# A new order of instructions for a three-stage attention, gMLP and expert-attention kernel, with k's high part copied twice from PSUM and scaled weight words on either of two engines

## The chip, the cores and the metric

One core of one Trainium2 chip runs the program. The metric is the device time of one execution in microseconds (us). Engines are named as in the profile: PE is TensorE (matmuls and transposes), DVE is VectorE, ACT is ScalarE, POOL is GpSimd, SP is SyncE, which issues every load and store here.

## What is computed

Three stages run one after the other on a batch of 4 sequences of 576 positions with 512 features (8 heads of 64):

```python
# (a) attention in a window of 64 positions
scores = scale * np.matmul(q, k.transpose(0, 1, 3, 2))
mask = (rel >= 0) & (rel < window)          # rel = query position - key position
attn = softmax(np.where(mask, scores, -1e9)); x = attn @ v
# (b) gated MLP with a mix over positions
h = np.maximum(x @ w_in, 0.0); u, v = h[..., :512], h[..., 512:]
v_n = (v - mu) / np.sqrt(var + 1e-06)
v_s = np.einsum('ts,bsd->btd', w_spatial, v_n) + b_spatial[None, :, None]
x = (u * v_s) @ w_out
# (c) four experts, causal attention each (head 64); each position keeps its two best by logits
logits = x @ w_gate; w = normalised exp of the two best logits, 0 for the others
for e in range(4):
    a = softmax(causal(scale * (x @ wq[e]) @ (x @ wk[e]).T)); out += w[e] * (a @ (x @ wv[e]) @ wo[e])
```

Inputs and output are float32. The kernel splits many operands into a high and a low part (names ending in h and l: xh and xl, woh and wol, kd with kz for k) and adds two or three matmuls for one product.

## The kernel before

**The planner.** The code first describes the work as nodes: an engine (or several that could do it, with a cost on each), a function that emits the instructions, the nodes it depends on, and the tiles that it allocates and uses. A class `Planner` (`N = plan.node`) is a list scheduler: in `run` it goes forward in planned time, and whenever an engine is free it starts there the ready node of lowest priority number. Priorities are running sums of work, moved by the table `SHIFT`, one number for each unit of work and kind (PE, other engines, loads). `SWITCH` is a penalty for changing between full-array and tiled matmuls on PE; `DVE_BIAS`, `POOL_BIAS` and `EFT` decide which engine takes a node that several could do; `RATE` is the planned speed of loads; `CLASH` makes DVE and POOL wait for each other in the plan where both work in SBUF (`sbuf=True`). The costs are only for planning. The resulting order is written out as it stands: each engine executes its list in order and waits by semaphores. All loads and stores stand on SP's queue.

**Two plans.** Phase 1 holds (a), (b) and the folding of w_out into the weights of (c); phase 2 holds (c). Each ends in `plan.run()`. Phase 2 begins in PE's queue some 280 us after the start.

**The front.** Stage (a) goes by couples of score units. PE multiplies scores into a bank of PSUM (`s_mm`, matmuls of 64x128, first operands vt, ut or kt); DVE adds the mask and takes the extremum (`s_top`, L546, into pa, and mx for the row values); ACT exponentiates (`s_exp`, L552); DVE adds and inverts (L568, L570); DVE, POOL or ACT multiply by the inverse (`s_norm`, L558 on ACT, L560 otherwise); PE transposes (`p_t`, L564, "T" below); ACT or DVE copy the result to SBUF (pt); PE multiplies by v (`pv`, pt with woh and wol, or with vt, into a bank); ACT or DVE write xh, DVE subtracts for xl (L357). When all xh and xl of 128 positions are there, PE can do a b_v unit (12 matmuls of 128x512, `w,xh` and `w,xl`: v of the MLP). Four of these and a short one for the last 64 positions stand in the front, then the first b_u unit (`xh,w`, 128x288). From there PE has matmuls of stage (b) ready at all times.

**Weights.** The helper `prep64` takes weights as pairs of 32-bit words: `down` scales one word into a bank (L679, ACT), `sign` masks it (L674 and L676), and DVE shifts and joins (L688 to L696); then a copy makes the high part and a subtraction the low part.

**Dummies.** PE's first instructions are `WARM` dummy matmuls (`heat`, ident by ident, each leaves two records in the trace), and 60 single ones (`FILL`) have the worst priority, so that the planner puts one wherever it finds nothing else for PE. There are 68 with `WARM = 8`.

**Phase 2.** `c_qk` makes q and k of an expert: `hi` copies each half of k's high part from PSUM to kd, `lo` subtracts for the low part, and `twin` copies kd once more to the other half of the partitions (64x288 each). `c_v` makes v and, with it, the gate's logits (`w,xh` 128x260, "gate-and-v unit" below). `unit` is a block of causal softmax: scores (`kd,qs` and `kz,qs`), L1207 on DVE, exponent on ACT (L1218), L1220 to L1222 on DVE or POOL (p times the inverse and the gate), transposes on PE (L1238) and a copy to pg. `c_pv` multiplies by v, and `c_wo` by wo, copies the bank to a tile of ot, of which there are three, and stores it. For one block (`b == B - 1 and t == 1`) it does this in two halves of 256 columns. The layernorm of (b) has its small steps at L766 to L772.

## Time and profile before

| what | value |
|---|---|
| time, median of 3 runs | 447.91 us (447.51 to 448.07) |
| the profiled execution | 448.94 us, its span 447.1 us |
| PE busy | 438.9 us (98%), 3962 matmul records |
| DVE busy | 310.9 us (70%) |
| ACT busy | 293.1 us (66%) |
| POOL busy | 107.4 us (24%) |
| clock granted to PE | full (1.00) over the whole span |

The span runs from the first instruction to the last landing; the profiled execution's time has 1.84 us around it. An engine's busy share is a mean over stages that differ, so the rows below go by stretches. A timeline row begins with its start in us and its length; in brackets stands how long the engine idled before it and what ended the idling. Rows that follow each other on an engine can overlap, as instructions are pipelined.

### The profile page before, as it was taken

Reading aid. Unit: us, or ns where it says so; the run is one execution under the profiler, and the core shown is the slowest. Engines: PE = TensorE matmul, PEld = TensorE weight load, DVE = VectorE, ACT = ScalarE, POOL = GpSimd, SP = SyncE. Lnnn points to the kernel's source line nnn. Section 1 sums busy time; section 2 is a strip of 40 time slices with the busy share of each in tenths; the row PEclk is TensorE's granted clock in tenths of the full one; section 3 lists DMA queues with packets and bytes.
Section 4 is the critical chain, followed back from the end, with each engine's and each line's share of the span. In section 5 each row is a group of like instructions: output and inputs, shape, how many; then the busy total and the mean of one; then the engine's idle time right before and its main releaser. Section 6 shows DMA issues by size and latency. Waiting matters only on the chain.

```text
span 447.1 us, 10829 instructions
## 1 busy us (share of the span) xinstructions
PE 438.9 (98%) x3962; PEld 396.0 (89%) x3962; DVE 310.9 (70%) x1241; ACT 293.1 (66%) x926; POOL 107.4 (24%) x154
## 2 busy tenths in 40 slices
PE   8999999999999999999999999999999999999996
PEld 7977899989899879998899999789899978897875
DVE  4989989962875988024544556998697987787650
ACT  4989989662676969203322346987675978777863
POOL 4335782400310126000200251610031011011110
PEclk9999999999999999999999999999999999999999
DMA  7994837140242605003001000000010001000114
GB/s 280 281 330 122 251 101 221 45 140 0 64 138 64 179 7 144 0 1 95 1 1 48 0 1 1 1 2 1 1 48 25 1 2 48 0 2 25 71 53 160
DMA packets 31079, 33.10 MB, mean 74 GB/s; under 512 B 1905, under 2 KB 24689, under 8 KB 31026
## 3 DMA queue, kind: packets, MB, share of 16 engines
q1 hardware_dynamic: 31026, 32.41, 23.4%
q8 instruction: 31, 0.51, 0.5%
q14 instruction: 22, 0.18, 0.1%
HBM read 27.68 MB, written 4.72 MB: 72 GB/s over the span
## 4 chain that ended last, share of the span: by engine, by line
PE 87%; DVE 6%; ACT 4%; issue 2%; POOL 1%; POOLq 0%; ACTq 0%; DVEq 0%
PE bank L333 79%; PE bank L1238 5%; PE bank L564 3%; DVE p L1207 1%; ACT pa L552 1%; DVE qs L357 1%; POOL p L1222 1%; DVE p L1222 1%; ACT p L1218 1%; DVE pa L546 0%; ACT pa L558 0%; DVE pa L560 0%; DVE kz L357 0%; ACT pg L344 0%; ACT kd L344 0%
## 5 line engine op out<-in xcount | busy, mean ns | idle before, releaser
L333 PE MATMUL bank<-xh,w 128*128 128x288 f32 x512 | 109.6, 298 | 0.0
L333 PEld LDWEIGHTS bank<-xh,w 128*128 128x128 f32 x512 | 84.1, 188 | 0.9 <-DVE st L767 0.2
L333 PE MATMUL bank<-xl,w 128*128 128x288 f32 x256 | 75.3, 294 | 0.0
L333 PE MATMUL bank<-w,xh 128*128 128x512 f32 (+1 forms) x256 | 64.7, 342 | 0.2 <-ACT pt L344 0.2
L552 ACT ACTIVATE pa<-pa,mx 128x128 f32<-128x128 f32 x144 | 55.9, 400 | 5.4 <-DVE mx L546 5.4
L333 PEld LDWEIGHTS bank<-xl,w 128*128 128x128 f32 x256 | 48.2, 188 | 0.4
L333 PEld LDWEIGHTS bank<-w,xh 128*128 128x128 f32 x256 | 43.2, 188 | 5.7 <-ACT pt L344 0.5
L1218 ACT ACTIVATE p<-p,mc 128x128 f32<-128x128 f32 (+4 forms) x72 | 41.8, 582 | 8.4 <-DVE mc L1207 7.7
L1222 POOL TENSOR_SCALAR p<-p,mc,fx 128x256 f32<-128x256 f32 (+4 forms) x26 | 17.1, 658 | 111.3 <-DVE mc L1221 52.2
L333 PE MATMUL bank<-w,xl 128*128 128x512 f32 (+1 forms) x128 | 43.2, 338 | 0.0
L333 PE MATMUL bank<-wsp_h,vh 128*128 128x288 f32 x128 | 38.6, 302 | 0.0
L333 PE MATMUL bank<-wsp_h,vl 128*128 128x288 f32 x128 | 37.7, 295 | 0.0
L333 PE MATMUL bank<-wsp_l,vh 128*128 128x288 f32 x128 | 37.7, 294 | 0.0
L1207 DVE CUSTOM_DVE_ANT_0 p<-bank,cmask 128x128 f32<-128x128 f32 (+4 forms) x72 | 33.2, 482 | 5.2 <-PE bank L333 4.2
L770 POOL TENSOR_TENSOR st<-st,nhalf 128x1 f32<-128x1 f32 (+1 forms) x20 | 12.3, 615 | 98.7 <-DVE st L769 98.7
L344 ACT ACTIVATE pg<-bank 128x128 f32<-128x128 f32 (+4 forms) x71 | 29.1, 440 | 5.2 <-PE bank L1238 4.7
L546 DVE CUSTOM_DVE_ANT_0 pa<-bank,mask 128x128 f32<-128x128 f32 x120 | 28.4, 284 | 5.9 <-POOL mx L415 4.1
L1238 PE MATMUL bank<-ident,p 128*128 128x128 f32 x192 | 30.1, 278 | 1.5 <-POOL p L1222 0.7
L333 PE MATMUL bank<-kd,qs 128*128 128x128 f32 (+5 forms) x96 | 30.5, 335 | 0.0
L552 ACT ACTIVATION_READ_ACCUMULATOR pa<-pa,mx 128x1 f32 x144 | 28.6, 199 | 0.0
L333 PE MATMUL bank<-kz,qs 128*128 128x128 f32 (+5 forms) x96 | 28.4, 313 | 0.0
L835 DVE TENSOR_TENSOR y<-bank,ut 128x288 f32<-128x288 f32 x24 | 10.9, 454 | 24.9 <-PE bank L333 24.9
(209 smaller groups left out, 1083.4 us busy)
## 6 DMA issues: line engine op xcount, KB each, us to landing
vt<-in_v_dram SPq DMA_DIRECT2D x12, 512.0 KB, 4.9
qa<-in_qT_dram SPq DMA_DIRECT2D x44, 96.0 KB, 3.8
out_dram<-ot SPq DMA_DIRECT2D x15, 256.0 KB, 2.0
y<-in_w_in_dram SPq DMA_DIRECT2D x7, 512.0 KB, 7.3
kt<-in_kT_dram SPq DMA_DIRECT2D x12, 288.0 KB, 5.0
y<-in_w_outT_dram SPq DMA_DIRECT2D x4, 512.0 KB, 4.5
y<-in_wspT_dram SPq DMA_DIRECT2D x2, 576.0 KB, 4.2
vt<-in_kq_dram SPq DMA_DIRECT2D x2, 384.0 KB, 4.4
```

Of the source, the lines that this page charges most:

```text
L333: pe.matmul(o, lhsT, rhs, start=start, stop=stop)
L344: act.activation(o, i, AF.Copy)
L357: engs[e].tensor_tensor(out=o, in0=a, in1=hi.bitcast(F32), op=ALU.subtract)
L546: dve.tensor_tensor_reduce(out=pa[:, j, :], in0=ps[:, j * 128:(j + 1) * 128], in1=mask(j), scale=-0.125, scalar=3.0e38, op0=ALU.add, op1=A ...
L552: act.activation(pa[:, j, :], pa[:, j, :], AF.Exp, bias=mx[:, j, 0:1], scale=-1.0, accum_out=mx[:, j, 1:2])
L564: pe.transpose(ps2[:, j * 128:(j + 1) * 128], pa[:, j, :], ident)
L770: a = N((POOL, 464), lambda e: pool.tensor_tensor(out=st[:m, 9:10], in0=st[:m, 8:9], in1=nhalf[:m], op=ALU.pow), [n1], use=[st])
L835: dve.tensor_tensor(out=o, in0=ps[:, :HS], in1=u[:, d, tk], op=ALU.mult)
L1207: dve.tensor_tensor_reduce(out=P[:, a0:a1], in0=ps[:, :w], in1=msk, scale=-0.125, scalar=3.0e38, op0=ALU.add, op1=ALU.min, accum_out=mc[:, ...
L1218: a = N((ACT, 284 + 0.87 * L), lambda e: act.activation(P[:m, :L], P[:m, :L], AF.Exp, bias=mc[:m, 0:1], scale=-1.0, accum_out=mc[:m, 2:3]) ...
L1222: a = N({POOL: 328 + 0.832 * L, DVE: 90 + 0.52 * L}, lambda e: engs[e].tensor_scalar(P[:, :L], P[:, :L], mc[:, 3:4], fx[:, I, ev:ev + 1], ...
L1238: pe.transpose(ps[:, j * m:(j + 1) * m], P[:, j * 128:(j + 1) * 128], ident)
```

## The change

- Tables and constants: `SHIFT` (all numbers), `SWITCH`, `DVE_BIAS`, `POOL_BIAS`, `EFT`, `RATE` (360 to 328) are replaced, `WARM` goes from 8 to 4, and some planning costs (the first `s_mm`, `s_norm`, a `tensor_reduce`) and `sbuf` flags of the plan change. None of these alters an instruction; they alter the order, the engine that takes a node, and the number of dummies.
- `twin` reads k's high part from the PSUM bank (ps) where it read kd in SBUF.
- `down` may also run on DVE, as a `tensor_scalar` with two multiplications.
- In the layernorm the operation that negates the mean (L769 before) is gone; the last operation subtracts the mean where it added its negative.

```diff
-SWITCH = 107920.0
+SWITCH = 147606.0
...
-DVE_BIAS = (1136.0, 1147.0)
-POOL_BIAS = (1131.0, 1068.0)
-WARM = 8
+DVE_BIAS = (156.0, 2438.0)
+POOL_BIAS = (1196.0, -5786.0)
+WARM = 4
...
-EFT = (636.0, 778.0)
+EFT = (1480.0, 9505.0)
...
-    ISSUE, WAY, RATE, FLIGHT = 475.0, 650.0, 360.0, 8
+    ISSUE, WAY, RATE, FLIGHT = 475.0, 650.0, 328.0, 8
...
-        S_N[n0] = S_N[n0 + 1] = top = N((PE, 816), s_mm, kn + [Q_N[n0], Q_N[n0 + 1], S_N.get(n0 - 1)], alloc=bank, use=hk, prio=prio,
+        S_N[n0] = S_N[n0 + 1] = top = N((PE, 816 if n0 else 1500), s_mm, kn + [Q_N[n0], Q_N[n0 + 1], S_N.get(n0 - 1)], alloc=bank, use=hk, prio=prio,
...
-            a = N({POOL: 1053, DVE: 450, ACT: 880}, s_norm, [a], use=[pa, mx], prio=prio, sbuf=True)
+            a = N({POOL: 955, DVE: 468, ACT: 880}, s_norm, [a], use=[pa, mx], prio=prio, sbuf=True)
...
         def down(e):
-            act.activation(fb.t, word(1).bitcast(F32), AF.Copy, scale=2.0 ** -112)
+            if e == ACT:
+                act.activation(fb.t, word(1).bitcast(F32), AF.Copy, scale=2.0 ** -112)
+            else:
+                dve.tensor_scalar(fb.t, word(1).bitcast(F32), 2.0 ** -112, 1.0, op0=ALU.mult, op1=ALU.mult)
...
-        n1 = N((ACT, 550), down, [n0], alloc=[fb], use=[raw], prio=prio)
+        n1 = N({ACT: 550, DVE: 602}, down, [n0], alloc=[fb], use=[raw], prio=prio)
...
-        n2 = N((DVE, 70), lambda e: dve.tensor_scalar(st[:m, 10:11], st[:m, 6:7], -1.0, None, op0=ALU.mult), [a], use=[st])
...
         a = N({DVE: 460, POOL: 850}, lambda e: engs[e].tensor_scalar(
-            vr[:m], vr[:m], st[:m, 10:11], st[:m, 9:10], op0=ALU.add, op1=ALU.mult), [a, n2], use=[vr, st], sbuf=True)
+            vr[:m], vr[:m], st[:m, 6:7], st[:m, 9:10], op0=ALU.subtract, op1=ALU.mult), [a], use=[vr, st], sbuf=True)
...
             def twin(e):
                 for x in range(2):
-                    copy(e, kd[x][HALF[1 - x], tk], kd[x][HALF[x], tk])
+                    copy(e, kd[x][HALF[1 - x], tk], ps[HALF[x], :HS])
...
-            n3 = N(halves(HS, False), twin, [n1], use=kd, sbuf=True)
+            n3 = N(halves(HS), twin, [n1], use=[ps] + kl + kd)
```

What the tables do shows in the instructions. On PE the real units are the same, 68 dummies become 64. Ahead of the fourth b_v unit PE has nine groups of scores (24 matmuls each), 14 transposes and 64 of the dummies before, ten groups, 14 transposes and 61 dummies now; behind it, up to the first b_u unit, none before and three now. Over the whole program the softmax norms of (a) go from 25 on DVE, 16 on ACT (48 operations) and 7 on POOL to 17, 14 and 17; DVE's copies out of PSUM and in SBUF go from 37 to 97 and ACT's fall from 382 to 310; `down` goes from 12 on ACT to 9 there and 3 on DVE; the copies of kd out of kd on ACT (32) become copies out of the bank. Three places:

**The front.** On PE, from the second group of scores on, before; the rows of `bank<-ident` are dummies, x10 is ten of them, and L564 are the transposes of the softmax:

```order
L333 MATMUL bank_66<-ident 128x128 x10
L564 MATMUL bank_72<-ident,pa 128x128 x3
L564 MATMUL bank_73<-ident,pa 128x128 x3
L333 MATMUL bank_66<-ident 128x128 x10
L333 MATMUL bank_67<-pt,woh 64x64 x12
L333 MATMUL bank_66<-ident 128x128 x5
L564 MATMUL bank_71<-ident,pa 128x128 x3
L333 MATMUL bank_66<-ident 128x128 x3
```
and now:

```order
L333 MATMUL bank_66<-ident 128x128 x3
L564 MATMUL bank_71<-ident,pa 128x128 x3
L333 MATMUL bank_66<-ident 128x128 x14
L564 MATMUL bank_68<-ident,pa 128x128 x3
L333 MATMUL bank_66<-ident 128x128 x3
L564 MATMUL bank_70<-ident,pa 128x128 x3
L564 MATMUL bank_71<-ident,pa 128x128 x3
L333 MATMUL bank_66<-ident 128x128
L333 MATMUL bank_73<-pt,woh 64x64 x12
L333 MATMUL bank_68<-pt,wol 64x64 x12
L333 MATMUL bank_66<-ident 128x128
```
Before, the dummies are spread in groups of ten, ten, five and three, and a product with v (pt) follows the second transpose; now 14 stand behind the first transpose, and the product follows the fourth. POOL's first instructions of the front, before (L560 is a norm of the softmax, L357 a subtraction for a low part, L346 a copy for a high part, L674 a sign mask):

```order
L357 TENSOR_TENSOR w<-w_251,w 128x512
L346 TENSOR_SCALAR w<-y_288 128x512
L357 TENSOR_TENSOR w<-y_288,w 128x512
L357 TENSOR_TENSOR w<-y_313,w 128x512
L357 TENSOR_TENSOR w<-y_393,w 128x512
L560 TENSOR_TENSOR pa<-pa,mx_123 128x384
L770 TENSOR_TENSOR st<-st,nhalf 128x1
L772 TENSOR_SCALAR vr<-vr,st 128x512
L674 TENSOR_SCALAR y_601<-y_461 128x512
L357 TENSOR_TENSOR vl<-vr,vh 128x512
L560 TENSOR_TENSOR pa<-pa,mx_126 128x384
```
and now:

```order
L560 TENSOR_TENSOR pa<-pa,mx_123 128x384
L560 TENSOR_TENSOR pa<-pa,mx_124 128x384
L346 TENSOR_SCALAR w<-y_258 128x512
L357 TENSOR_TENSOR w<-y_258,w 128x512
L357 TENSOR_TENSOR w<-w_292,w 128x512
L357 TENSOR_TENSOR w<-y_345,w 128x512
L560 TENSOR_TENSOR pa<-pa,mx_126 128x384
L357 TENSOR_TENSOR w<-y_407,w 128x512
L560 TENSOR_TENSOR pa<-pa,mx_122 128x384
L346 TENSOR_SCALAR w<-y_494 128x512
L357 TENSOR_TENSOR w<-y_494,w 128x512
```
Four norms stand among POOL's first eleven operations, where there were two, and two of them ahead of every piece of weights. Up to the last xl that the fourth b_v unit needs there are six norms on POOL now, and two before.

**The change of phase.** On PE, where the first softmax of phase 2 is transposed (L1238 before, L1241 now), before; `kd,qs` with `kz,qs` is a QK unit, `w,xh` with `w,xl` of 128x260 a gate-and-v unit, `pg,v` a product with v:

```order
L333 MATMUL bank_69<-kz_3560,qs 128x512
L1238 MATMUL bank_66<-ident,p 128x128
L333 MATMUL bank_71<-kd,qs 128x384
L333 MATMUL bank_71<-kz_3560,qs 128x384
L1238 MATMUL bank_72<-ident,p 128x128
L1238 MATMUL bank_68<-ident,p 128x128 x2
L333 MATMUL bank_66<-kd,qs 128x288
L333 MATMUL bank_66<-kz_3560,qs 128x288
L333 MATMUL bank_66<-kd,qs 64x288
L333 MATMUL bank_66<-kz_3559,qs 64x288
L1238 MATMUL bank_67<-ident,p 128x128 x2
```
and now:

```order
L333 MATMUL bank_69<-w,xl 128x260
L1241 MATMUL bank_71<-ident,p 128x128
L333 MATMUL bank_67<-kd,qs 128x512
L333 MATMUL bank_67<-kz_3531,qs 128x512
L1241 MATMUL bank_69<-ident,p 128x128
L333 MATMUL bank_71<-w,xh 128x260 x2
L333 MATMUL bank_71<-w,xl 128x260
L333 MATMUL bank_71<-w,xh 128x260 x2
L333 MATMUL bank_71<-w,xl 128x260
L333 MATMUL bank_71<-w,xh 128x260 x2
L333 MATMUL bank_71<-w,xl 128x260
L333 MATMUL bank_71<-w,xh 128x260 x2
```
Before, seven QK units and one unit of q stand ahead of the first transpose (the seventh is the first row shown); now nine QK units and a gate-and-v unit do (its last row is the first one shown), one more gate-and-v unit stands between the second transpose and the third, and two more behind it.

**The tail.** ACT's last copies from the banks to ot, each followed by its store on SP, before:

```order
L344 ACTIVATE ot<-bank_69 128x512
L344 ACTIVATE oh<-bank_66 128x256
L344 ACTIVATE ot<-bank_73 128x512
L344 ACTIVATE ot<-bank_67 128x256
L344 ACTIVATE ot<-bank_72 128x256
L344 ACTIVATE ot<-bank_71 128x512
L344 ACTIVATE ot<-bank_70 128x512
L344 ACTIVATE ot<-bank_68 128x512
L344 ACTIVATE ot<-bank_69 128x512
```
and now:

```order
L344 ACTIVATE ot<-bank_69 128x512
L344 ACTIVATE ot<-bank_72 128x512
L344 ACTIVATE oh<-bank_67 128x256
L344 ACTIVATE ot<-bank_66 128x512
L344 ACTIVATE ot<-bank_73 128x512
L344 ACTIVATE ot<-bank_68 128x512
L344 ACTIVATE ot<-bank_70 128x256
L344 ACTIVATE ot<-bank_71 128x256
```
The block that is done in two halves of 128x256 stood before the last four full ones; now its halves are the last. The one before them holds the last 64 positions of two sequences, and leaves by two stores.

## Rows read from the trace of the kernel before

**Rows 1.** Windows: stretch, its length; busy us (instructions) of PE, PEld, DVE, ACT, POOL; clock.

```profile
0.00:46.00 46.00, 42.84 (x516) 37.25 (x518) 37.65 (x170) 37.35 (x140) 21.01 (x44) 1.00 0.79 252
...
100.00:280.00 180.00, 180.00 (x1661) 168.46 (x1660) 101.20 (x373) 88.12 (x288) 32.21 (x52) 1.00 0.16 46
280.00:300.00 20.00, 19.23 (x143) 16.65 (x143) 19.34 (x84) 17.59 (x54) 9.48 (x10) 1.00 0.01 2
...
sum 447.00, PE 438.87 PEld 396.00 DVE 310.95 ACT 293.09 POOL 107.42; mean PE 48.76 PEld 44.00 DVE 34.55 ACT 32.57 POOL 11.94
```
**Rows 2.** Windows, from the first softmax operation to the fourth b_v unit.

```profile
7.09:48.66 41.57, 39.98 (x550) 34.46 (x548) 38.59 (x171) 38.73 (x147) 16.67 (x22) 1.00 0.81 256
```
**Rows 3.** Timeline of PE: scores (vt) and dummies (ident) near the start.

```profile
5.28 1.55 PE L333 MATMUL bank<-vt 64*64 64x128 f32 x24
...
8.07 0.89 PE L333 MATMUL bank<-vt 64*64 64x128 f32 x24
...
8.89 2.50 PE L333 MATMUL bank<-ident 128*128 128x128 f32 x20
```
**Rows 4.** Timeline of PE, the front: two transposes, and the fourth b_v unit's first matmuls.

```profile
24.99 0.55 PE L564 MATMUL bank<-ident,pa 128*128 128x128 f32 x3 [0.89 <-DVE pa L560]
...
44.86 0.55 PE L564 MATMUL bank<-ident,pa 128*128 128x128 f32 x3 [0.48 <-ACT pt L344]
...
48.66 0.73 PE L333 MATMUL bank<-w,xh 128*128 128x512 f32 x2
```
**Rows 5.** Timeline of DVE, the front: scores (L546) and norms (L560).

```profile
7.09 0.29 DVE L546 CUSTOM_DVE_ANT_0 pa<-bank,mask 128x128 f32<-128x128 f32 x1 [4.12 <-POOL mx L415]
...
10.86 0.56 DVE L560 TENSOR_TENSOR pa<-pa,mx 128x384 f32<-128x384 f32 x1
...
23.45 1.48 DVE L560 TENSOR_TENSOR pa<-pa,mx 128x384 f32<-128x384 f32 x1
...
40.05 1.70 DVE L560 TENSOR_TENSOR pa<-pa,mx 128x384 f32<-128x384 f32 x1
...
48.44 0.28 DVE L546 CUSTOM_DVE_ANT_0 pa<-bank,mix 128x128 f32<-128x128 f32 x1
```
**Rows 6.** Timeline of POOL, the front: subtractions.

```profile
23.25 1.27 POOL L357 TENSOR_TENSOR w<-y,w 128x512 fp32r<-128x512 f32 x1 [2.82 <-ACT w L344]
...
48.21 1.29 POOL L357 TENSOR_TENSOR vl<-vr,vh 128x512 fp32r<-128x512 f32 x1 [2.04 <-ACT vh L344]
```
**Rows 7.** Groups by line and form, whole span: count, busy us, mean ns, idle before.

```profile
L344 ACT ACTIVATE kd<-kd 64x288 fp32r<-64x288 f32 x32 | 14.1, 440 | 0.5
...
L344 ACT ACTIVATE kd<-bank 64x288 fp32r<-64x288 f32 x30 | 12.1, 403 | 7.1 <-PE bank L333 6.5
L560 DVE TENSOR_TENSOR pa<-pa,mx 128x384 f32<-128x384 f32 x25 | 18.3, 731 | 0.4
...
L688 DVE SCALAR_TENSOR_TENSOR y<-y,bank 128x512 int32<-128x512 int32 x3 | 2.1, 687 | 0.0
L560 POOL TENSOR_TENSOR pa<-pa,mx 128x384 f32<-128x384 f32 x7 | 6.7, 964 | 34.4 <-ACT pa L558 20.7 <-DVE mx L570 8.2 <-ACT pa L552 5.5
```
**Rows 8.** Timelines of PE, DVE and POOL around 290 us.

```profile
290.25 0.55 PE L1238 MATMUL bank<-ident,p 128*128 128x128 f32 x3 [0.51 <-DVE mc L1220]
...
288.83 1.37 DVE L1222 TENSOR_SCALAR p<-p,mc,fx 128x384 f32<-128x384 f32 x1
...
288.56 2.91 POOL L357 TENSOR_TENSOR xl<-y,xh 128x576 fp32r<-128x576 f32 x2
```
**Rows 9.** Timeline of the end: ACT's copies to ot and PE's last matmul.

```profile
436.70 0.60 ACT L344 ACTIVATE ot<-bank 128x512 f32<-128x512 f32 x1 [1.18 <-PE bank L333]
...
440.36 1.17 ACT L344 ACTIVATE ot<-bank 128x512 f32<-128x512 f32 x2 [1.80 <-DMA out_dram<-ot]
...
443.19 0.40 PE L333 MATMUL bank<-w,ol 128*128 128x512 f32 x1
443.68 0.60 ACT L344 ACTIVATE ot<-bank 128x512 f32<-128x512 f32 x1 [0.78 <-PE bank L333]
```

More of the change, by code (lines that the diff above doesn't have):

```diff
@@ L1149, in lead, with N_ @@
             return m1(n)[:, :, None].to_broadcast(s3)
-        def N_(c, f, deps, alloc=()):
-            return N((DVE, c), lambda e: f(), deps, alloc=alloc, use=[] if alloc else [ex, ga, gb])
+        def N_(c, f, deps, alloc=(), sbuf=True):
+            return N((DVE, c), lambda e: f(), deps, alloc=alloc, use=[] if alloc else [ex, ga, gb], sbuf=sbuf)
         tt, tr_ = dve.tensor_tensor, dve.tensor_reduce
-        n1 = N_(90, lambda: tr_(out=m1(0), in_=lg, axis=AX.X, op=ALU.max), LG_N[b], [ex, ga, gb])
+        n1 = N_(90, lambda: tr_(out=m1(0), in_=lg, axis=AX.X, op=ALU.max), LG_N[b], [ex, ga, gb], False)
         n2 = N_(155, lambda: tt(out=gt(), in0=lf, in1=le, op=ALU.is_gt), [n1])
@@ L1160, in c_gate @@
         n4 = N((ACT, 210), lambda e: act.activation(ex.t, ex.t, AF.Exp), [n4], use=[ex])
-        nf = N_(0, lambda: None, [n2, n3, n4])
+        nf = N_(0, lambda: None, [n2, n3, n4], sbuf=False)
         n2 = N_(155, lambda: tt(out=gt(), in0=gt(), in1=eq(), op=ALU.add), [n2, n3])
-        n2 = N_(150, lambda: tr_(out=rk(), in_=gt(), axis=AX.X, op=ALU.add), [n2])
+        n2 = N_(150, lambda: tr_(out=rk(), in_=gt(), axis=AX.X, op=ALU.add), [n2], sbuf=False)
         n2 = N_(80, lambda: dve.tensor_scalar(rk(), rk(), 1.5, None, op0=ALU.is_lt), [n2])
         n2 = N_(90, lambda: tt(out=ex.t, in0=ex.t, in1=rk(), op=ALU.mult), [n2, n4])
-        n2 = N_(90, lambda: tr_(out=m1(1), in_=ex.t, axis=AX.X, op=ALU.add), [n2])
+        n2 = N_(90, lambda: tr_(out=m1(1), in_=ex.t, axis=AX.X, op=ALU.add), [n2], sbuf=False)
         n2 = N_(70, lambda: dve.tensor_scalar(m1(1), m1(1), 1e-9, None, op0=ALU.add), [n2])
-        n2 = N_(75, lambda: dve.reciprocal(m1(1), m1(1)), [n2])
+        n2 = N_(75, lambda: dve.reciprocal(m1(1), m1(1)), [n2], sbuf=False)
         n4 = N_(90, lambda: tt(out=ex.t, in0=ex.t, in1=lead(1), op=ALU.mult), [n2])
@@ L1215, in unit @@
         if len(parts) == 2:
-            tops = [N((DVE, 70), lambda e: dve.tensor_reduce(out=mc[:m, 0:1], in_=mc[:m, 0:2], axis=AX.X, op=ALU.min), tops, use=[mc], prio=prio)]
+            tops = [N((DVE, 75), lambda e: dve.tensor_reduce(out=mc[:m, 0:1], in_=mc[:m, 0:2], axis=AX.X, op=ALU.min),
+                      tops, use=[mc], prio=prio)]
         a = N((ACT, 284 + 0.87 * L), lambda e: act.activation(P[:m, :L], P[:m, :L], AF.Exp, bias=mc[:m, 0:1], scale=-1.0,
```

6 rows, old and new, of the table SHIFT are left out of this document.

## The prediction

> **What bounds the kernel now.** I read the windows view first, which cuts the span into stretches and gives each engine's busy time [rows 1]. TensorE (PE) is busy 438.87 us of 447; from 100 to 280 us it is busy all 180.00. A stretch like that cannot be shortened by making another engine faster, only by giving PE less to do. PE's idle time sits in four places: the first 46 us (46.00 - 42.84 = 3.16), the change of phase at 280 to 300 us (20.00 - 19.23 = 0.77), the end, where only the last copies and stores are left, and 0.8 us scattered between.
>
> The front needs a second look, because "busy" there includes 64 of the 68 dummy matmuls (ident by ident) that the planner puts where nothing else is ready. From 7.09 us, when VectorE (DVE) starts the first softmax, to 48.66 us, where the fourth and last b_v unit begins, DVE is busy 38.59 of 41.57 us and ScalarE (ACT) 38.73: both 93% [rows 2]. So the front runs at the pace of these two, and PE's dummies only colour the waiting. PE's timeline shows the waits that still got through [rows 4]: 0.89 us for a softmax norm on DVE at 24.99, 0.48 for a copy on ACT at 44.86. The profiled execution took 448.94 us, a span of 447.1 and 1.84 around it; that is 1.03 above the median of 447.91. I make the sum against 448.94 and subtract 1.03 at the end. What a measurement of this kernel can tell from no change is taken as 0.2%, 0.9 us.
>
> **The edits that the diff shows, priced.** The order on PE holds the same real units. The edits of single instructions are small and mostly covered:
> - The copies that double k's high part read PSUM, no longer SBUF. On ACT the nearest rows are 440 ns from SBUF and 403 ns from PSUM [rows 7], so 32 copies give ACT back 32 x 0.037 = 1.2 us. They lie nearly all in the stretch that PE fills without a gap [rows 1], so I take 0; bounds -0.5 (should they be what the change of phase waits for) and 0. The read keeps a PSUM bank longer by one copy, 0.4 us, which could hold a unit of PE back only where all eight banks are full; taken as 0, bound +0.4 once at the change of phase.
> - The scaled words: in the order, 3 of 12 move from ACT to DVE. DVE's nearest row, an operation of 128x512 in the same helper, is 687 ns [rows 7]; 3 x 0.69 = 2.1 us more for DVE, one of them in the front. Bounds 0 and +0.7 there; it is in the front's sum below.
> - 20 tiny DVE operations (the mean times -1) go. They stand between larger ones and cover 20 x 0.07 = 1.4 us of DVE over 450 us, of which one in four is in the front: 0 to -0.3 there.
> - The planner's rate of loads, its costs and its tables change no instruction by themselves: they act through the order.
>
> **The order: four terms.**
>
> *Dummies.* 68 become 64, all on PE's path if PE is never kept waiting. Ten of them, in 20 records, take 2.50 us at 8.89 [rows 3], so one takes at most 0.25; I take 0.23, as the row's end includes the last one's drain: 4 x 0.23 = -0.9. But fewer at the start bring the softmax no forward step: its first operation on DVE waits for GpSimd's (POOL's) memset of mx until 7.09 [rows 5], whereas the first scores already run at 5.28 [rows 3]. Bounds -0.9 and 0. Ahead of the fourth b_v unit three dummies fewer (61 for 64) stand against one more group of scores, 8.89 - 8.07 = 0.82 [rows 3]: PE reaches that unit at the same time, within 0.2, if it never waits.
>
> *Front.* Here DVE has more to do. Counting its instructions in the order up to the last one that the fourth b_v unit needs, at the mean of their forms, I get 33.9 us before and 36.2 now (more scores and five copies of the transposed softmax out of PSUM, which ACT did, but three norms fewer); ACT goes from 34.9 to 32.7. These two sums are estimates of mine. From 38.59 busy and 2.98 idle [rows 2], 2.3 more would put the unit 2.3 late. Against that stand DVE's collisions with POOL: its norm takes 0.56 us alone (10.86), but 1.48 at 23.45, while POOL did a subtraction from 23.25 on, and 1.70 at 40.05 [rows 5, 6], together 2.06 us lost. Four of the norms ahead of that unit go to POOL (6 there, for 2). Without collisions the front would be 2.3 - 2.06 = +0.2; with the same two, +2.3. And part of the 2.98 idle can go: where I add up each engine's work to the instruction that PE needs next, and compare it with PE's own work up to there, the tightest place now leaves DVE 2.8 us; before it was 1.7, at the wait of 0.89. I take +0.3, nearer the low end; bounds -1.6 (the 41.57 - 39.98 us that PE idles in that stretch [rows 2]) and +3.4 (both collisions, two more, and nothing of the idle).
>
> The Trainium skill has a rule on this, in SBUF — State Buffer, "Who interferes with whom": VectorE and GpSimd share one pair of ports under an exclusive lock that is held for a whole instruction, and only a VectorE operation with two inputs in SBUF, or in a two-port mode, needs it. The trace agrees: a score operation, which reads PSUM, took its usual 0.28 us at 48.44 in the middle of POOL's subtraction of 48.21 [rows 5, 6]. By the rule a norm that moves to POOL takes a claimant off the lock, and the front would come out at +0.2, not +2.3.
>
> *Change of phase.* Before, PE waits 0.51 us at 290.25 for a transposed softmax, whose norm on DVE took 1.37 us beside POOL's two subtractions of 2.91 us together [rows 8]. The new order puts nine QK units and a whole gate-and-v unit ahead of the first softmax transpose, and three more of those units among the next few transposes (each twelve matmuls that need no softmax). So the 0.77 us of PE's idle there [rows 1] should go: -0.8. Bounds 0 (later transposes wait in their place) and -0.8 for idle, -1.7 if starts that were pushed apart without a listed wait close up too.
>
> *Tail.* The last unit is now half as wide. Its copy on ACT is of 128x256, where 128x512 took 0.60 us [rows 9]; with a half to the whole of that as bounds I take 0.4: -0.2. Against it: the three tiles of ot. At 440.36 a copy waited 1.80 us for a store to leave its tile; that tile had been filled from 436.70 to 437.30, so it was 3.06 us from fill to free [rows 9]. In the new order the last copy takes the tile filled three copies earlier, whose matmuls end about 2.8 us before its own (a full unit and two halves); filled 0.7 later and free 3.06 after that, it would be free 1.0 after the last matmul, where the copy could begin at 0.1 (443.68, where the last record ended at 443.59). Wait 0 to 0.9, I take 0.4: together +0.2, bounds -0.3 and +0.9. PE's total in the tail is the same.
>
> Rest of the second phase: taken as 0, bounds -0.8 (all idle left over) and +0.8.
>
> **Sum.** -0.9 + 0.3 - 0.8 + 0.2 = -1.2: 447.7 for a profiled execution, 446.7 for the median.
>
> **The rivals.**
> - *As forecast*, 445.5 to 447.0: the dummies and the change of phase pay, the front does not answer. For it: the same PE units in both. Chance 0.40.
> - *More gain*: with the norms off DVE the front's waits go too (-1.6), the change of phase closes up (-1.7), the tail gives -0.2: -0.9 - 1.6 - 1.7 - 0.2 = -4.4, 443.5. For it: 2.06 us of collisions in the front. Against it: 93% on DVE and 2.3 us more for it. Chance 0.17.
> - *No change*, 447.0 to 448.8: the order gives up 1.5 to 2 us in the front, DVE with the same two collisions (+2.3) and a little of its idle back (-0.5): -0.9 + 1.8 - 0.8 + 0.2 = +0.3, 448.2. Also where PE waits for DVE in the front, the dummies saved there were never on the path. Chance 0.25.
> - *Slower*: the collisions multiply. POOL has 17 norms for 7, 964 ns each [rows 7], and DVE more conversions in SBUF; one collision costs 0.92 to 1.14 us (1.48 or 1.70 less 0.56). DVE has 2.8 us in hand in the front; from the third collision more than before, PE waits. Four more, less the half hidden by dummies, and a transition that gains nothing: -0.9 + 3.4 + 0 + 0.2 = +2.7, 450.6. For it: DVE's 25 norms average 731 ns, against 0.56 alone [rows 7, 5], 25 x 0.17 = 4.3 us already lost. Chance 0.18.
>
> **How the numbers follow.** Faster by over 0.2% (below 447.0): 0.40 + 0.17 = 0.57. Within 0.2%: 0.25. Slower (above 448.8): 0.18. The likeliest case alone gives 446.7, and 445.5 to 447.0. The range for 8 in 10 takes in half of the large gain, from 443.7, and half of the slower case, to 449.5.
>
> **What would show it.** Right: the fourth b_v unit starts at 48.4 to 49.3 us with three dummies after it; PE's idle at 280 to 300 below 0.3; the last copy of ot a 128x256 that waits for a store by under 0.9; the chain of waits still over 85% PE. Wrong: idle before L564's matmuls in the front of over 2 us, released by DVE (the collisions; then DVE's and POOL's norms would average over 0.8 and 1.05), or PE's idle in the second phase spread over several waits for POOL's norms of p.

## The result and the profile after

The changed kernel takes 454.23 us (median of 4 runs, 454.16 to 454.45); the kernel before took 447.71 in 4 runs beside it (447.5 to 448.07). The ratio is 1.0146 with a 95% interval of 1.0128 to 1.0163: slower by 6.5 us, where 1.2 us less were forecast and the range ended at 449.5.

The profiled execution's span is 452.4 us. Its windows answer to [rows 1] (stretch, length; busy us of PE, PEld, DVE, ACT, POOL; clock):

```profile
0.00:46.00 46.00, 44.25 (x595) 38.32 (x596) 39.44 (x187) 36.25 (x138) 27.84 (x52) 1.00 0.90 281
46.00:100.00 54.00, 51.89 (x571) 46.07 (x568) 49.02 (x207) 38.82 (x145) 34.23 (x34) 1.00 0.45 140
100.00:280.00 180.00, 178.83 (x1603) 168.40 (x1602) 101.43 (x348) 75.36 (x233) 38.52 (x52) 1.00 0.15 43
280.00:300.00 20.00, 19.05 (x144) 17.95 (x142) 15.72 (x66) 15.93 (x45) 8.47 (x8) 1.00 0.01 2
...
433.00:452.40 19.40, 15.51 (x105) 11.26 (x103) 4.48 (x19) 6.68 (x16) 0.45 (x1) 1.00 0.32 100
sum 452.40, PE 439.46 PEld 395.24 DVE 322.26 ACT 267.34 POOL 132.94; mean PE 48.83 PEld 43.92 DVE 35.81 ACT 29.70 POOL 14.77
```
Before, the stretch of 46 to 100 us, which [rows 1] leave out, was

```profile
46.00:100.00 54.00, 54.00 (x613) 49.49 (x608) 46.27 (x185) 43.62 (x152) 25.19 (x24) 1.00 0.50 152
```
PE does as much as before (439.46 us for 438.87) and its clock is as it was. What grew is its idle time. The first 46 us got better (1.75 idle for 3.16), but the two stretches that were full, 46 to 100 and 100 to 280, now have 2.11 and 1.17 us of idling; the change of phase has 0.95 for 0.77. DVE and POOL do more, ACT does less. PE's waits, by what it waited for (us in all, times, longest), begin so, after the one before its first matmul:

```profile
PE bank L1241 <- POOL p L1225: 1.5, 3, 1.1
PE bank L333 <- DMA vt<-in_v_dram: 1.2, 1, 1.2
PE bank L564 <- POOL y L674: 0.8, 1, 0.8
PE bank L333 <- ACT kd L344: 0.7, 1, 0.7
```
None of these waits is longer than 1.2 us. Much of the loss is not listed as waiting at all: units start later than the shortest spacing of such units allows. So I read from PE's timeline where three marks stand, the first b_u unit, the first QK unit and the last matmul's end, and took the lengths between them:

| kernel | first b_u | first QK | last end | b_u to QK | QK to end |
|---|---|---|---|---|---|
| before | 53.39 | 279.52 | 443.59 | 226.1 | 164.1 |
| changed | 53.51 | 282.55 | 448.50 | 229.0 | 166.0 |

By these marks phase 1 behind the front is 2.9 us longer, phase 2 1.9, and what follows the last matmul 0.4 (452.4 - 448.50 = 3.9, where it was 3.5). But the marks do not part the same work in both orders. A unit of q, twelve matmuls of 128x288, stands behind the first QK unit before (281.25 to 282.85) and ahead of it now, so 1.6 us of PE's work have changed sides. With the same work on either side, phase 2 is 3.5 us longer (166.0 + 1.6 - 164.1). Ahead of the first b_u unit the new order has some 1.3 us more work, an estimate from the spacing of these units in the traces (two more groups of scores at 0.82, six transposes at 0.11 and a product with v at 0.85, less the short b_v unit at 1.85).

In executions of three other kernels with before's order the front was 1.3 to 1.5 us shorter than in the one shown (first b_u at 51.93, 51.98 and 52.09: `before_twin`, `before_warm4` and `before_late4` below); the profiled execution stands 1.03 above the median of 447.91. With the 1.3 us of moved work taken off, the new front (53.51) is 1.2 us shorter than the one shown and 0.1 to 0.3 longer than those three. Up to the first QK unit, with the unit of q taken off, the changed kernel needs 280.95 us: 1.4 more than the execution shown, 2.9 more than two of the three (278.02 and 278.04; the third, without four dummies, is left out). And 2.9 + 3.5 + 0.4 = 6.8 is near the 6.5 us between the medians, so before's median seems to go with the short front.

### The profile page after: what moved, and what is told of

Its sections match the earlier page's. It is cut to its first block, busy times and chain, and to the rows that moved or that the text cites. A ratio compares the mean times of both kernels' runs of the same rounds, so it can differ in the third digit from the quotient of the medians.

```text
span 452.4 us, 10834 instructions
## 1 busy us (share of the span) xinstructions
PE 439.5 (97%) x3954; PEld 395.2 (87%) x3954; DVE 322.3 (71%) x1284; ACT 267.3 (59%) x835; POOL 132.9 (29%) x178
## 4 chain that ended last, share of the span: by engine, by line
PE 70%; DVE 14%; ACT 8%; issue 3%; POOL 2%; DMA 2%; DVEq 0%; ACTq 0%; POOLq 0%
PE bank L333 64%; PE bank L1241 3%; DVE p L1209 3%; PE bank L564 3%; ACT kd L344 2%; ACT pa L552 2%; DVE p L1225 2%; DVE kz L357 2%; DMA vt<-in_v_dram 1%; ACT p L1221 1%; DVE pg L348 1%; DVE xl L357 1%; DVE mc L1224 1%; DVE qs L357 1%; DVE xh L348 1%
## 5 line engine op out<-in xcount | busy, mean ns | idle before, releaser
L1225 POOL TENSOR_SCALAR p<-p,mc,fx 128x128 f32<-128x128 f32 (+4 forms) x32 | 21.1, 662 | 118.5 <-DVE mc L1224 46.3
L1221 ACT ACTIVATE p<-p,mc 128x128 f32<-128x128 f32 (+4 forms) x72 | 41.8, 582 | 13.4 <-DVE mc L1209 10.1
L1241 PE MATMUL bank<-ident,p 128*128 128x128 f32 x192 | 30.6, 278 | 2.7 <-POOL p L1225 1.5
L546 DVE CUSTOM_DVE_ANT_0 pa<-bank,mask 128x128 f32<-128x128 f32 x120 | 28.2, 284 | 4.8 <-POOL mx L415 4.1
L333 PE MATMUL bank<-kd,qs 128*128 128x384 f32 (+5 forms) x96 | 30.3, 332 | 0.9 <-ACT kd L344 0.7
L769 DVE BATCH_NORM_STATS2 st<-vr 128x6 f32<-128x512 f32 (+1 forms) x20 | 13.8, 688 | 24.1 <-ACT vr L352 23.9
L344 ACT ACTIVATE kd<-bank 64x288 fp32r<-64x288 f32 x60 | 24.3, 405 | 9.5 <-DVE kz L357 4.0
L1241 PEld LDWEIGHTS bank<-ident,p 128*128 128x128 f32 x192 | 22.0, 140 | 7.5 <-POOL p L1225 3.5
L333 PE MATMUL bank<-kz,qs 128*128 128x384 f32 (+5 forms) x96 | 28.3, 312 | 0.0
```

Source lines behind the costliest of these rows:

```text
L333: pe.matmul(o, lhsT, rhs, start=start, stop=stop)
L344: act.activation(o, i, AF.Copy)
L546: dve.tensor_tensor_reduce(out=pa[:, j, :], in0=ps[:, j * 128:(j + 1) * 128], in1=mask(j), scale=-0.125, scalar=3.0e38, op0=ALU.add, op1=A ...
L769: a = N((DVE, 600), lambda e: dve.bn_stats(st[:m, 0:6], vr[:m]), [a], alloc=[st], use=[vr])
L1221: a = N((ACT, 284 + 0.87 * L), lambda e: act.activation(P[:m, :L], P[:m, :L], AF.Exp, bias=mc[:m, 0:1], scale=-1.0, accum_out=mc[:m, 2:3]) ...
L1225: a = N({POOL: 328 + 0.832 * L, DVE: 90 + 0.52 * L}, lambda e: engs[e].tensor_scalar(P[:, :L], P[:, :L], mc[:, 3:4], fx[:, I, ev:ev + 1], ...
```

## Experiments

Each kernel is one of the two with few lines changed; unless said otherwise the plan, and so the order of every engine's instructions, stays as it was, because only what a node emits is altered.

### The subtraction in the layernorm, undone and alone

`after_add`: the changed kernel with the negated mean and the addition back.

```diff
-        n1 = N((DVE, 70), lambda e: dve.tensor_scalar(st[:m, 8:9], st[:m, 7:8], 1e-6, None, op0=ALU.add), [a], use=[st])
+        def eps_neg(e):
+            dve.tensor_scalar(st[:m, 8:9], st[:m, 7:8], 1e-6, None, op0=ALU.add)
+            dve.tensor_scalar(st[:m, 10:11], st[:m, 6:7], -1.0, None, op0=ALU.mult)
+        n1 = N((DVE, 70), eps_neg, [a], use=[st])
...
-            vr[:m], vr[:m], st[:m, 6:7], st[:m, 9:10], op0=ALU.subtract, op1=ALU.mult), [a], use=[vr, st], sbuf=True)
+            vr[:m], vr[:m], st[:m, 10:11], st[:m, 9:10], op0=ALU.add, op1=ALU.mult), [a], use=[vr, st], sbuf=True)
```

> The changed kernel, in its own order, with the negated mean and the addition in the layernorm put back (20 tiny operations on VectorE more, the last layernorm operation adds where it subtracted). Theory 'slow subtract': GpSimd's layernorm operation goes back from 2.08 us to about 0.77, 6 times, 7.9 us less on GpSimd, and TensorE's waits at 65 to 82 us shrink: 452.0 to 453.2 us. Theory 'order alone': the waits come from which work stands behind which, and the six long operations are covered: 454.2, within 0.4.

`before_sub`: the kernel before with the opposite edit: its last operation subtracts, and the node of the negation emits nothing.

> The kernel before, in its own order, with the layernorm's last operation subtracting the mean and the 20 tiny operations left out. Theory 'slow subtract': GpSimd's ten take 2.08 us for 0.77 to 1.37, 12 us more on GpSimd in the first 230 us, and TensorE waits for some of them: 448.5 to 450.5. Theory 'order alone': within 0.4 of 447.7.

Measured: `after_add` 453.41 us (452.70, 452.74, 454.09, 454.16), `before_sub` 452.24 (451.42 to 452.45; ratio 1.0079, 1.0058 to 1.0100). The operation on POOL, in groups by line and form, is first in the kernel before, then in `before_sub`, then in `after_add`:

```profile
L772 POOL TENSOR_SCALAR vr<-vr,st 128x512 f32<-128x512 f32 x7 | 6.4, 909 | 0.8
```
```profile
L772 POOL TENSOR_SCALAR vr<-vr,st 128x512 f32<-128x512 f32 x7 | 15.2, 2165 | 0.7
```
```profile
L777 POOL TENSOR_SCALAR vr<-vr,st 128x512 f32<-128x512 f32 x3 | 2.3, 776 | 0.3
```
So on POOL a subtraction and a multiplication of 128x512 by two values per row take 2.1 us where an addition and a multiplication take 0.8 to 0.9 on the mean. In before's order ten of these make the kernel 4.1 us slower, which is beyond the theory's 0.8 to 2.8. In its profile the first QK unit starts at 282.72 for 279.52, and phase 2 is 164.1 long as before: all of the loss is in phase 1. There ACT's copies to vh wait longer for POOL's results, before and in `before_sub`:

```profile
ACT vh L344 <- POOL vr L772: 0.7, 2, 0.6
```
```profile
ACT vh L344 <- POOL vr L772: 4.8, 4, 1.6
```
In the new order, with six on POOL, taking them away gives little: two of the four executions are as long as those of the changed kernel, two 1.5 us shorter, and the profile, which is of one of the long two, has PE's last matmul end at 448.38 us for 448.50. What parts the two pairs is, as far as the profiles show, another thing, a late load (below). The median lies between the ranges of the two theories. The theory of the slow subtraction holds for one order, and in the other at most 0.3 us are left for it (see "Together").

### The second copy of k, undone and alone

`after_twin_sbuf` is the changed kernel, `before_twin` the kernel before, each with this line as the other has it (in `before_twin` the node also holds the bank, which leaves the order as it is):

```diff
-                    copy(e, kd[x][HALF[1 - x], tk], ps[HALF[x], :HS])
+                    copy(e, kd[x][HALF[1 - x], tk], kd[x][HALF[x], tk])
```

> The changed kernel, in its own order, with the second copy of k's high part read from SBUF as before. Theory 'bank': reading the bank ties ScalarE to VectorE's subtraction on the same bank (five waits of ScalarE, 4.0 us, in the trace of the changed kernel, one of which holds TensorE for 0.7 us); without it 453.0 to 453.6. Theory 'order alone': the copy costs ScalarE 37 ns more each and nothing else changes: 454.2 to 454.6.

> The kernel before, its order unchanged on every engine, with the second copy of k's high part read from the PSUM bank, as the change has it. Theory 'bank' (ScalarE's copy and VectorE's subtraction of the same bank are made to wait for each other): 448.5 to 450.5 against 447.9. Theory 'only in the new order' (the wait costs where the new order puts the copy behind the subtraction): within 0.5 of 447.9. The diff's own arithmetic (37 ns less for each copy): 447.4.

Measured: `after_twin_sbuf` 450.53 us (450.24 to 451.67), 3.7 less than the changed kernel; `before_twin` 451.09 (450.57 to 452.38; ratio 1.0075, 1.0056 to 1.0094), 3.3 more than the kernel before. Both orders agree, both differences are larger than the theory of the bank had them, and the sign is the opposite of the 37 ns that the shorter copy gives. The timelines of the changed kernel on ACT, DVE and PE show how:

```profile
299.69 0.82 ACT L344 ACTIVATE kd<-bank 64x288 fp32r<-64x288 f32 x2
...
302.48 0.82 ACT L344 ACTIVATE kd<-bank 64x288 fp32r<-64x288 f32 x2 [1.35 <-DVE kz L357]
```
```profile
301.53 0.92 DVE L357 TENSOR_TENSOR kz<-bank,kd 64x288 fp32r<-64x288 f32 x2
```
```profile
303.36 0.40 PE L333 MATMUL bank<-kd,qs 128*128 128x288 f32 x1 [0.72 <-ACT kd L344]
```
ACT has made kd at 299.7. DVE subtracts for kz from the same bank at 301.53 and is done at 302.45, and only then ACT starts the second copy out of that bank, having idled 1.35 us; a QK unit on PE waits 0.72 us for it. In `after_twin_sbuf` the same pair, on ACT and DVE:

```profile
297.99 0.83 ACT L344 ACTIVATE kd<-bank 64x288 fp32r<-64x288 f32 x2 [0.23 <-PE bank L333]
...
299.47 0.91 ACT L344 ACTIVATE kd<-kd 64x288 fp32r<-64x288 f32 x2
```
```profile
299.39 0.92 DVE L357 TENSOR_TENSOR kz<-bank,kd 64x288 fp32r<-64x288 f32 x2
```
The copy (299.47) and the subtraction (299.39) run at the same time. The wait is in the program: of ACT's instructions in the order, with what each waits for, the pair reads

```
changed:          ACTIVATE kd<-bank_67 64x288 [waits DVE_49]
after_twin_sbuf:  ACTIVATE kd<-kd 64x288 [waits Activation_49] x2
```

Where the copy stands ahead of the subtraction, it is DVE that waits. What ended the idle time of the engines ahead of their work on kd (us, times), in the kernel before, in `before_twin` and in the changed kernel:

```profile
  PE bank L333: 6.5, 8
  ACT kd L344: 4.8, 3
```
```profile
  ACT kd L344: 13.4, 10
  PE bank L333: 6.3, 7
  DVE kz L357: 3.0, 4
```
```profile
  ACT kd L344: 7.9, 11
  DVE kz L357: 4.0, 5
```
Before, DVE waited for ACT's kd 3 times, 4.8 us; in `before_twin` 10 times, 13.4 us, and ACT for DVE 4 times besides. More work on DVE costs time in phase 2 (`after_p_dve` below), and here phase 2 grows by 3.1 us (167.2 from the first QK unit to the end). The Trainium skill says why the wait must be there: by PSUM — Partial Sum Buffer, "PSUM bank collisions raise a hardware error", two engines must not be on one bank in the same quadrant of 32 partitions at once, not even both reading. No run here lets them collide; the semaphores and the waits agree with it.

### Both edits in either order

`before_edits` is the kernel before with both edits, `after_add_twin` the changed kernel without both.

> The kernel before, in its own order, with both edits of instructions at once: the layernorm subtracts the mean (20 tiny operations left out) and the second copy of k's high part reads the bank. Theory 'the edits make the loss': 4.1 and 3.3 us add up, as one acts in phase 1 and the other at the change of phase and in phase 2: 454 to 456 us, as much as the whole change. Rival (they overlap): 451.5 to 453.

> The changed kernel, in its own order, without both edits (mean negated and added, second copy from SBUF). Theory 'the edits make the loss, the order nothing': 447.5 to 448.5. Theory 'the new order is itself slower by 2 to 3 us, and hides the slow subtraction': 450.0 to 450.7, as with the copy alone put back.

Measured: 455.11 us (454.15 to 455.73) and 450.59 (449.87 to 451.67). With the two kernels compared, this makes a square:

| | without the two edits | with them |
|---|---|---|
| before's order | 447.71 | 455.11 |
| the new order | 450.59 | 454.23 |

In before's order the edits cost 7.4 us, the sum of 4.1 and 3.3; in the new order 3.6. The order itself costs 2.9 us without them and gives 0.9 with them. So the second theory on `after_add_twin` is right: the new order has a loss of its own. The marks on PE's timeline, as above:

| kernel | first b_u | first QK | last end | b_u to QK | QK to end |
|---|---|---|---|---|---|
| before_twin | 51.93 | 278.02 | 445.23 | 226.1 | 167.2 |
| before_sub | 54.08 | 282.72 | 446.86 | 228.6 | 164.1 |
| before_edits | 54.63 | 283.12 | 450.17 | 228.5 | 167.1 |
| after_twin_sbuf | 53.54 | 281.26 | 444.52 | 227.7 | 163.3 |
| after_add_twin | 53.85 | 281.58 | 444.43 | 227.7 | 162.9 |

The copy lengthens phase 2 by 3.1 us in before's order (167.2 for 164.1) and by 2.7 in the new one (166.0 for 163.3), the subtraction phase 1 behind the front by 2.5 in before's order. The new order without the edits seems to have a phase 2 that is 1.2 us shorter than before's, but that is the unit of q, which stands ahead of the mark there: with the same work it is 0.4 longer (162.9 + 1.6 - 164.1). Its loss is in phase 1: without the unit of q the first QK unit would start at 279.98, 0.5 later than in the execution of before that is shown and 2.0 later than where before's front was the shorter one (278.02).

### The late load

In the changed kernel PE waits once for a load of v, issued at 129.80 us (timelines of PE and SP):

```profile
135.06 0.57 PE L333 MATMUL bank<-pt,vt 128*64 128x64 f32 x12 [1.17 <-DMA vt<-in_v_dram]
```
```profile
129.80 0.38 SPq L426 DMA_DIRECT2D vt<-in_v_dram  x1
```
From issue to landing this load took 5.2 us. In `after_twin_sbuf`, whose order is the same up to here and whose load goes out at 129.90, it took 3.5 us, and PE does not wait:

```profile
133.42 0.92 PE L333 MATMUL bank<-pt,vt 128*64 128x64 f32 x24
134.26 0.89 PE L333 MATMUL bank<-kt,qa 64*64 64x128 f32 x24
```
`twin_vsplit` is `after_twin_sbuf` with each such load issued as two, the three blocks that are needed first ahead.

```diff
-        KV_N["v", b, p] = load(..., lambda: dma(hv.t, windows(b, 0, 8, slice(p * 128, (p + 1) * 128))), ...
+        KV_N["v", b, p] = load(..., lambda: [dma(hv[:, i:i + n, :], windows(b, i, n, slice(p * 128, (p + 1) * 128))) for i, n in ((0, 3), (3, 5))], ...
```

> The changed kernel with the second copy from SBUF, and each load of v for the window attention issued as two, its first three blocks ahead of the other five (12 issues more). Theory 'late load' (the load issued at 129.8 us lands 1.2 us after TensorE could have used it, in some executions and not in others): 449.9 to 450.4 in every execution, where the same kernel with whole loads went from 450.2 to 451.7. Rival (the spread has another source): the median stays at 450.5 or above and the executions spread by 1.4 us again.

Measured: 450.58 us, 450.27 to 450.71. The spread is 0.4 us where whole loads gave 1.4, and no execution is in the upper group, as the theory had it; the executions lie up to 0.3 us above its range, and the median is where the rival put it. Four executions alone do not prove it, but the profiles agree: in the new order those of executions in an upper group show PE waiting for a load of v (0.9 to 1.2 us, in the changed kernel, `after_add`, `twin_pt`, `order_xh` and `order_all`; `after_p_dve` below shows it too), those in a lower group do not (`after_twin_sbuf`, `after_add_twin`, `twin_norm`). So the late load is most likely what parts the groups. The median of 450.53 was already one of the lower group, so the median did not move. Compared group by group, the changed kernel (all four executions in the upper one) stands against 451.4 and 451.7 of `after_twin_sbuf`: the second copy is worth 2.7 us, the load 1.2. That all four executions of the changed kernel have the late load is taken from one profile and from their spread of 0.3 us.

### Which engine does it

Five kernels move work to another engine at its place in the order. `after_p_dve`: the changed kernel, all multiplications of p in phase 2 on DVE. `twin_norm` and `twin_pt`: `after_twin_sbuf` with POOL's softmax norms on DVE, and with DVE's copies of pt on ACT. `order_xh` and `order_all`: `after_add_twin` with the copies of xh and xt on ACT, and with pt and two relus too. The edits all read like these:

```diff
-                    engs[e].tensor_tensor(out=pa.t, in0=pa.t, ...
+                    dve.tensor_tensor(out=pa.t, in0=pa.t, ...
...
-                a = N(on_copy(w), lambda ...: copy(e, xh[:, cs], ps3[:, ss]), ...
+                a = N(on_copy(w), lambda ...: copy(ACT, xh[:, cs], ps3[:, ss]), ...
```

> The changed kernel, in its own order, with all 32 of GpSimd's multiplications of p in the second phase done by VectorE at the same place in the order. Theory 'GpSimd's latency': TensorE's transposes wait for GpSimd (1.5 us in three waits, 1.1 the longest, at 388 us); VectorE takes 0.5 us where GpSimd takes 0.7 and needs no semaphore, so 452.5 to 453.5. Theory 'VectorE is the tight one in the second phase' (it is busy 75 to 88% there): 15 us more work for it cost more than they give, 455 to 458.

> The changed kernel with the second copy from SBUF, and GpSimd's 17 norms of the window softmax moved to VectorE at their place in the order. Theory of the prediction's slower rival (norms on GpSimd, 0.9 us each, collide with VectorE and make TensorE wait): without them 448.5 to 450. Theory 'VectorE is the tight engine': 17 x 0.56 = 9.5 us more for it, of which TensorE waits for 2 to 5: 452.5 to 456.

> The changed kernel with the second copy from SBUF, and the 12 copies of the transposed softmax out of PSUM that VectorE does moved to ScalarE at their place in the order. Theory 'VectorE is the tight engine at 46 to 100 us' (it is busy 49.0 of 54 us there, 46.3 before; ScalarE 38.8, before 43.6): 6.6 us less for it, and TensorE's waits of some 3 us at 65 to 82 us shrink: 448.5 to 449.8 against 450.5. Rival (those waits are ScalarE's or a matter of the order): 450.2 to 452.

> The changed kernel in its own order, without both edits (450.6 us), and with the copies of xh and xt out of a bank all on ScalarE, as nearly all were before (24 of them are on VectorE in the new order). Theory 'one bank, two engines': where the order gave one of a bank's copies to VectorE and the other to ScalarE, they wait for each other (8 of 24 on the two engines at xt alone), and TensorE's waits of 65 to 82 us go in part: 448.8 to 449.8. Rival (the load of VectorE or the mere sequence): 450.2 to 451.2.

> As order_xh, and the copies of pt and the two relus of phase 1 on ScalarE too, as before; VectorE is back to its load of before in phase 1 (some 20 us less than in the new order), ScalarE too. Theory 'it is which engine has the work': 447.5 to 449. Rival 'it is the sequence in which the work stands', which stays: 450 to 452.

Measured: `after_p_dve` 458.30 us, 4.1 more; DVE's load in phase 2 (window 280 to 448, columns as above) is

```profile
280.00:448.00 168.00, 160.88 (x1171) 138.78 (x1170) 141.85 (x577) 114.44 (x317) 11.22 (x9) 1.00 0.06 22
```
141.85 us, where the changed kernel has 132.37. `twin_norm` 454.28, 3.7 more than 450.53. `twin_pt` 451.02 (449.59 to 451.48), no difference from 450.53 that its spread lets one tell. `order_xh` 451.10 (450.39 to 451.93) and `order_all` 452.60 (452.04 to 453.53), where 450.59 is the base. So DVE can take less than POOL, in both phases; but giving its copies of phase 1 back to ACT where they stand does not help either, and giving all of them back makes it 2 us slower. So the two theories that blamed the choice of engine for these copies are refuted. What is left is above all the sequence; not moved back were the three `down` on DVE, the norms that DVE and ACT gave to POOL (all 17 on DVE is another choice than before's), and phase 2's copies (30 of pg on DVE for 9). Part of the sequence's cost is seen: the late load in some executions, and waits at 65 to 82 us, 1.4 us in four waits in `after_add_twin`, of which PE's timeline shows

```profile
76.33 0.84 PE L564 MATMUL bank<-ident,pa 128*128 128x128 f32 x6 [0.56 <-DVE xl L357]
...
79.09 1.62 PE L333 MATMUL bank<-pt,vt 128*64 128x64 f32 x48 [0.30 <-DVE mx L546]
```
(the first for a bank that DVE reads). Why these come so late I have not taken apart further.

### The dummies, and a faster version

`before_late4`: the kernel before without its last four dummies. `before_warm4`: the kernel before with four dummies at the start where it has eight. `before_late4_xh`: the first, with five copies of xh and xt on ACT.

```diff
+    left = [FILL - 4]
+    def few():
+        left[0] -= 1
+        if left[0] >= 0:
+            heat(1)
...
-        N((PE, 228.0), lambda e: heat(1), [a], use=[warm], prio=1e9)
+        N((PE, 228.0), lambda e: few(), [a], use=[warm], prio=1e9)
...
-    a = N((PE, 427.0 * WARM), lambda e: heat(WARM), alloc=[warm], prio=-1e9)
+    a = N((PE, 427.0 * WARM), lambda e: heat(WARM - 4), alloc=[warm], prio=-1e9)
```

> The kernel before without the four dummies that stand at 172 to 204 us, where TensorE is busy all the time. The prediction's term (a dummy on the path costs 0.23 us): 446.9 to 447.1 against 447.8. Rival (they stand where TensorE would have waited anyway): within 0.3.

> The kernel before with four dummies in place of eight at the very start. The prediction's term, taken for each dummy alike: 446.9. The prediction's own counter (the first softmax operation waits for GpSimd's memset until 7.09 us, whenever the scores come): within 0.3 of 447.8.

> The kernel before without the four dummies at 172 to 204 us (447.0 us) and with its five copies of xh and xt on VectorE moved to ScalarE. Theory 'one bank, two engines': 446.5 to 447.0. Rival: 447.0 to 447.5, as ScalarE is busy 93% in the front.

Measured: `before_late4` 447.00 us (11 runs, 446.38 to 447.30; ratio 0.9973, 0.9962 to 0.9984), `before_warm4` 448.30 (11 runs; 1.0010, 1.0002 to 1.0019), `before_late4_xh` 447.15 (12 runs; 0.9983, 0.9970 to 0.9995). Four dummies in a full stretch cost 0.7 us, a little less than the 0.9 of the prediction's term; those at the start give nothing back when left out (448.30 is 0.6 above, which is more than the 0.3 that was allowed for no change). `before_late4_xh` comes out as its rival said: moving the copies gives nothing. `before_late4` is faster than both kernels of this study, by 0.7 us and 7.2 us in the medians.

## Why the prediction was wrong

**The edits priced at nothing.** This is the step that failed. On the copies the prediction took "0; bounds -0.5 ... and 0", and +0.4 once for the held bank. In the new order the second copy costs 2.7 us. The prediction compared two durations, 440 and 403 ns, which both came out right (405 ns after); it did not ask what else reads that bank. The answer was in the code: the subtraction on DVE, in the function between the first copy and the second. The term "Rest of the second phase: taken as 0" failed with it: with the same work, phase 2 is 3.5 us longer.

On the layernorm it took "0 to -0.3", for 20 tiny operations less. It never priced the operation that replaced the addition, since a subtraction on POOL is in no row of before. It takes 2.08 us for 0.77 to 0.9:

```profile
L560 POOL TENSOR_TENSOR pa<-pa,mx 128x384 f32<-128x384 f32 x17 | 15.3, 905 | 40.5 <-DVE mx L570 33.0 <-ACT pa L552 6.7 <-ACT pa L558 0.9
...
L774 POOL TENSOR_SCALAR vr<-vr,st 128x512 f32<-128x512 f32 x3 | 6.2, 2080 | 0.3
```
```profile
L560 DVE TENSOR_TENSOR pa<-pa,mx 128x384 f32<-128x384 f32 x17 | 11.1, 654 | 0.3
...
L774 DVE TENSOR_SCALAR vr<-vr,st 128x512 f32<-128x512 f32 x13 | 7.6, 585 | 6.4 <-POOL st L772 6.4
```
(POOL, then DVE, where 585 ns is what it was.) In before's order this alone is 4.1 us; in the new order, with six for ten on POOL, the runs show 0.3 us at most. So it explains little of the 6.5 us, and the prediction was saved from it by the order.

**The offset, 1.03.** Wrong. The sum was made for a profiled execution, and 1.03 us were then taken off, because before's profiled execution stood that far above its median. The changed kernel's does not: 454.22 for a median of 454.23. The offset belonged to the long front of that one execution, and adds 1.0 to the miss.

**Dummies, -0.9.** About right in size, though the prediction did not say which four it meant. All 64 dummies of the changed kernel run ahead of the first b_u unit, as 64 of the 68 did before. What has gone are the four at 172 to 204 us, in a full stretch, and in before's order `before_late4` shows 0.7 us for these. That `WARM` is four smaller gives nothing, as `before_warm4` shows.

**Front, +0.3.** Right in size only against other executions than the one it was made for. The fourth b_v unit starts at 47.55 after a wait of 0.45 us, and has three dummies behind it. That is 1.1 us ahead of the 48.66 of [rows 4], and outside the 48.4 to 49.3 that the prediction names; against 47.20, 47.26 and 47.35 in `before_twin`, `before_warm4` and `before_late4` it is 0.2 to 0.35 later. The wait of 0.48 us for a copy on ACT at 44.86, which the prediction read [rows 4], is not in those three; that the size fits there is luck.

```profile
47.55 0.73 PE L333 MATMUL bank<-w,xh 128*128 128x512 f32 x2 [0.45 <-DVE xt L357]
```
The norms are shorter than before: on DVE 654 ns on the mean for 731 [rows 7], on POOL 905 for 964. The Trainium skill's rule on the shared ports (SBUF — State Buffer, "Who interferes with whom") would have fewer collisions with norms moved to POOL, and these means agree. But they do not show that the move is the reason, since in `twin_norm`, with all 34 norms on DVE, they take 644 ns there. By its time (3.7 us more) `twin_norm` shows that in this order the 17 are better on POOL. The slower rival, which ended on the right side, did so by a mechanism that did not happen.

**Stretches that were full.** The prediction said that the stretch of 100 to 280 us can only be shortened by giving PE less to do, and took 0 for the rest of the second phase. That a full stretch can be broken open by a new order, it had as no term. PE now idles 2.11 us at 46 to 100 us, and the 1.17 us at 100 to 280 are the late load.

**Change of phase, -0.8.** Wrong: 0.95 us of idling for 0.77. The second copies hold ACT and DVE just there: with them from SBUF the first transpose comes 4.55 us after the first QK unit, with them from the bank 5.22 (285.81 - 281.26 and 287.77 - 282.55, on PE's timelines). But also without them the idle does not go: `after_twin_sbuf` has 0.84 us of it at 280 to 300 us, of which 0.57 is a wait of the second transpose for DVE. So the gate-and-v units did not bring what was forecast.

**Tail, +0.2.** Right within 0.2. The last copy waited 0.36 us for a store to leave its tile, where 0.4 was taken:

```profile
445.80 0.60 ACT L344 ACTIVATE ot<-bank 128x512 f32<-128x512 f32 x1 [0.82 <-PE bank L333]
...
448.62 0.38 ACT L344 ACTIVATE ot<-bank 128x256 f32<-128x256 f32 x1 [0.36 <-DMA out_dram<-ot]
```
From the last matmul to the end it is 3.9 us for 3.5.

**Together.** Of the 6.5 us the runs give 2.7 to the second copy, 1.2 to the late load, and 2.3 to the rest of the new order (449.87 and 450.12, the executions of `after_add_twin` in the lower group, against 447.71). These make 6.2; the subtraction has at most the remaining 0.3. As the rest of the order also has the four late dummies less, worth 0.7, the sequence itself costs some 3.0, and by the marks most of that is in phase 1. What in it costs this stays open; that it is not the choice of engine for the copies of phase 1 is shown.

## What to carry to other kernels

Price an edit by who else is on the same buffer, not by its own duration: a copy that is 8% shorter cost some 3 us in two different orders, because it reads a PSUM bank that another engine also reads, and the two then wait for each other. An operation that the trace does not have (here a subtraction on POOL for an addition) has no price until it is measured, however alike it looks. And a full engine protects nothing against a new order: compare the old order with the edits and the new order without them, since the sum of the two need not be what the pair does. Where an order moves work across a mark, compare the same work, and ask of a profiled execution whether it is like the median one.

## What the runs showed of the hardware that was not expected

- On POOL, the operation that adds a value per row and multiplies takes 0.77 us alone, for 128x512 and for 64x512; with a subtraction in place of the addition 2.08, for both sizes. On DVE both take 0.55. Only this pair of operations was tried.
- A load of 512 KB issued at 129.8 to 129.9 us took 3.5 us to land in one profiled execution and 5.2 in another, whose order is the same up to there; in the second PE waited 1.17 us for it. That this is why kernels of this order have two groups of times some 1.3 us apart is likely, not proven.
